# Maxout inputs of five token groups by a 3x3x2 product scheme of 15 slots a half, with nine units' keys turned on TensorE

## The chip, the cores and the metric

The kernel runs on one core of one Trainium2 chip. The metric is the device time of one execution in microseconds (us). A core has five engines that run beside each other, each through its own instruction list in order: PE (TensorE, matrix products), DVE (VectorE), ACT (ScalarE), POOL (GpSimd) and SP (SyncE, which here issues most DMAs). They wait for each other through semaphores.

## The reference

An attention recurrence in float32 over 4 batches, 8 heads, 768 steps and 48 features a head; its result, as 3072 tokens of 384 features, goes through a maxout layer:

```
f = 1 / (1 + exp(-f_logit))
for t in range(S):
    state = f[:, :, t, :, None] * state + einsum('bhd,bhe->bhde', k[:, :, t], v[:, :, t])
    y[:, :, t] = einsum('bhd,bhde->bhe', q[:, :, t], state)
x = y.transpose(0, 2, 1, 3).reshape(3072, 384)
h = maximum(maximum(x @ w1, x @ w2), x @ w3)      # w1, w2, w3: 384 x 768
out = h @ w_out                                   # w_out: 768 x 384
```

## The kernel before

**Attention.** Tokens are taken in 24 units of 128 (64 steps of two batches). A main loop makes one iteration per unit. In it stand, for the next unit n, `scan(n)` (running products `r` of the gates, DVE), `after(n)` (`ends` and the scaled keys `kh = kt * r`, POOL), `before(n)` (the scaled queries `qh`, POOL), `carry(n)` (`state` times `ends`, POOL), and the PE products of unit n-1: `y`, the state product `a<-v_ld,ks`, the pair product `a<-qh,kh` and `y<-qh,state`. The state product wants the keys with the steps on the partitions: `ks`. Units 0 to 5 get it from four PE transposes and an ACT copy (`keys`), units 6 to 21 from 16 DVE transposes of 32x128 blocks (`keys_by_blocks`, L386).

**Maxout layer.** Four units make a group of 512 tokens, packed as `xT` (384 features on 3 blocks of 128 partitions, by 512). There are six groups; the diff counts them 0 to 5, the title 1 to 6. One weight matrix is subtracted from the other two and goes into a linear part, so that `h` is the larger of two products and zero, plus the linear part. Group 0 has its own code (`ffn_first`). Groups 1 to 5 run the generator `ffn(g, xT)`: first the inputs (`inputs_by_pairs`: two products, six column blocks of 128, three feature blocks, two token halves of 256), then the outputs (`outputs_by_pairs`, `h @ w_out` by another product scheme that wants sums of `hm`, made by `sums_of_hm` on POOL). A product of 128x128 by 128x256 in float32 is two PE instructions; `inputs_by_pairs` makes 33 slots of two such products each a group, and wants five sums of pieces of `xT` (`sums_of_x`, POOL), the first of them when its sixth slot comes.

**Order.** The program is recorded in hand order, and every engine keeps to it. The main loop calls `fill(part)` five times per iteration: it advances the first generator in `pending` by nominal costs until a budget is used up. `PART` divides a group's cost over the 20 calls of four iterations, so that inputs and outputs of group g run in the iterations of group g+1's units. In an iteration about 14 slots' worth of maxout work stands around the unit's own products. `store_late` issues the stores of the group before; their source is the buffer `o` (`o_four`). SP issues, in one list, the loads of `q`, `k`, `f`, `v`, the weight checks' `raw` pieces, the stores and the copies that finish `xT`; with 16x32 pieces a unit costs many issues.

Of the kernel before, what the change touches and what calls it, by code (L numbers as in the profile page):

```python
# [46 lines left out]
C = 64  # L47
# [8 lines left out]
def kernel(  # L56
# [33 lines left out]
    def fast():  # L90
        ctx = ExitStack()
        with ctx:
# [58 lines left out]
            BY_ROWS = 6  # L151
            v_tiles = [keep.tile([128, H, DP], FP32, name=f"v_ld{i}") for i in range(NLD)]
# [52 lines left out]
            placed = [keep.tile([128, NK, 2 * PIECE], U32, name=f"placed{i}") for i in range(3)]  # L205

            def new_raw(n=0):
                n = n % RAW - (RAW - RAW_KEPT)
                if n >= 0:
                    return placed[n // NK][:, n % NK]  # L210
                return work.tile([128, 2 * PIECE], U32, name="raw", bufs=RAW - RAW_KEPT)
# [56 lines left out]
            def check_load(n):  # L268
                src = pieces[n][1]
                if src.dtype != FP32:  # L270
                    raw[n] = new_raw()
                    a = pieces[n][0].shape[1]
                    nc.sync.dma_start(out=raw[n].rearrange("p (a c) -> p a c", a=a),
                                      in_=src.bitcast(U32).rearrange("(a p) c -> p a c", a=a))
# [101 lines left out]
            def keys_by_blocks(u, n):  # L376

                if BY_ROWS <= u < NU - 2:
# [229 lines left out]
            def outputs_by_pairs(g, hm, xT):  # L608
# [13 lines left out]
                else:  # L622
# [3 lines left out]
                    partial = [rests[:, 0], rests[:, 1], rests[:, 0]]  # L626
# [170 lines left out]
            def ffn_first(xT):  # L797
# [35 lines left out]
                made += [[lambda: mix(4)]] + [[lambda n=n: mix_in(n)] for n in range(2)]  # L833
# [10 lines left out]
            w_two = [t.bitcast(FP32) for t in placed[0:2]]  # L844
            w_sum = [w_in[2][:, n] for n in range(NK)]

            def mix_in(n, engine=nc.gpsimd):

                dst, x, y, op = ((w_sum[0], w_two[1][:, 0], w_two[1][:, 1], ALU.add),
                                 (w_sum[1], w_sum[0], w_two[0][:, 0], ALU.subtract),  # L850
                                 (w_two[1][:, 0], w_two[0][:, 0], w_two[1][:, 0], ALU.subtract),
                                 (w_sum[2], w_two[0][:, 1], w_sum[1], ALU.subtract))[n]
                engine.tensor_tensor(dst, x, y, op=op)
# [3 lines left out]
            two = lambda t: t.rearrange("q (j t) -> q j t", j=2)  # L857

            def sums_of_x(g):

                if g not in summed:
                    xT = packed[g]
                    X = lambda k, h: halves(xT, k, h)
                    t1, t2, t3, t4, t5 = (halves(xT, NK, 0), halves(xT, NK, 1), s_mix[0][:, HJ - 1],
                                          rests[:, 2, 0:HALF], s_mix[1][:, HJ - 1])
                    for dst, x, y in ((t1, X(0, 1), X(0, 0)), (t2, X(1, 1), t1), (t3, X(1, 1), X(0, 1)),
                                      (t4, X(1, 0), t2), (t5, X(2, 0), X(2, 1))):
                        nc.gpsimd.tensor_tensor(dst, x, y, op=ALU.subtract)
                    summed[g] = t1, t2, t3, t4, t5
                return summed[g]  # L870

            def inputs_by_pairs(g, hm, xT):
                X = lambda k, h: halves(xT, k, h)
                t1, t2, t3, t4, t5 = sums_of_x(g)
                s1, s2, s4 = w_sum
                s3 = w_two[1][:, 0]
                COST = 2 * HALF * COLUMN
                out = lambda n, h: hm[:, 2 * n:2 * n + 2, h * HALF:(h + 1) * HALF]
                first, u3 = rests[:, 0:2, 0:HALF], tops[:, 2:4, 0:HALF]
                A, B, U5 = {}, {}, {}  # L880

                def into(b, n, w, x, begin=False):
                    for j in range(2):
                        nc.tensor.matmul(b[:, j * HALF:(j + 1) * HALF], lhsT=w[:, (2 * n + j) * 128:(2 * n + j + 1) * 128],  # L884
                                         rhs=x, start=begin and j == 0, stop=True, skip_group_check=True)

                def plain(n):
                    B[n] = bank(True)
                    into(B[n], n, w_two[0][:, 1], X(1, 0), True)
                    yield COST  # L890
                    into(B[n], n, w_two[0][:, 2], X(2, 0))
                    nc.scalar.copy(out(n, 0), two(B[n]))
                    yield COST

                def start(n):
                    A[n] = bank()
                    into(A[n], n, w_two[0][:, 0], X(0, 0), True)
                    nc.scalar.copy(first, two(A[n]))
                    yield COST

                def join(n):
                    nc.gpsimd.tensor_tensor(out(n, 0), out(n, 0), first, op=ALU.add)

                def fifth(n):
                    into(B[n], n, s1, t1, True)
                    U5[n] = two(new_top(TOK))
                    nc.scalar.copy(U5[n], two(B[n]))
                    yield COST

                def sixth(n):  # L910
                    into(A[n], n, s2, t2)
                    nc.scalar.copy(out(n, 1), two(A[n]))
                    yield COST

                def seventh(n):
                    into(A[n], n, s3, t3)
                    yield COST
# [507 lines left out]
```

## Time and profile before

| | |
|---|---|
| median of three runs | 406.75 us (406.54, 406.75, 408.45) |
| span of the profiled execution | 403.7 us |
| outside the span, by the median | 3.05 us (the profiled execution's own time isn't listed) |
| PE busy | 390.9 us, 97% of the span |
| weight loads on PE (overlap its products) | 339.7 us, 84% |
| DVE busy | 297.7 us, 74% |
| POOL busy | 256.4 us, 64% |
| ACT busy | 180.9 us, 45% |

The span runs from the first to the last instruction of the core. The page gives it in 40 slices with the busy tenths of each engine and the granted clock of PE, then the chain of work that ended last, the costliest groups of instructions (busy time, mean ns of one, idle time ahead of them and what ended it) and the DMA issues. "SPq" is SP issuing a DMA: its time is that of the issue, and the landing is told apart. A matmul's end in the timeline is modelled and overlaps the next one's start; the distance of two starts is what one costs.

### The profile page before, as it was taken

How to read it: one execution, taken by the hardware profiler on the slowest of the kernel's cores; microseconds unless marked ns; L12 is line 12 of the kernel's file. 1: busy time of each engine (PE TensorE's matmuls, PEld its weight loads, DVE VectorE, ACT ScalarE, POOL GpSimd, SP SyncE). 2: the span in 40 equal slices, each digit the busy share in tenths (PEclk: the TensorE clock that was granted, in tenths of full speed). 3: DMA queues.
4: the chain of work that ended last, by engine and by line, in shares of the span. 5: the costliest groups of instructions: out<-in, count | busy, mean ns of one | idle time of the engine just before them, and what ended most of it. 6: DMA issues, size and time to landing. Idle time of an engine off the chain costs nothing.

```text
span 403.7 us, 11683 instructions
## 1 busy us (share of the span) xinstructions
PE 390.9 (97%) x4658; PEld 339.7 (84%) x4658; DVE 297.7 (74%) x572; ACT 180.9 (45%) x431; POOL 256.4 (64%) x283
## 2 busy tenths in 40 slices
PE   5988999999999999999999999999999999999995
PEld 4766765559998889998889988899988889988995
DVE  6997897999989999897998997998995450002600
ACT  3478787422224442345532344523354425586120
POOL 2189695879997697296587277667477850435700
PEclk9999999999999999999999999999999999999999
DMA  8999986767574576576635477634573003541002
GB/s 171 233 282 284 279 214 89 153 92 150 82 96 114 69 154 135 104 120 84 131 104 97 62 113 88 156 78 81 75 157 91 1 19 87 143 136 70 2 19 63
DMA packets 181611, 47.21 MB, mean 117 GB/s; under 512 B 160497, under 2 KB 179249, under 8 KB 181553
## 3 DMA queue, kind: packets, MB, share of 16 engines
q1 hardware_dynamic: 177536, 45.52, 54.7%
q10 hardware_dynamic: 4016, 0.91, 1.1%
q8 instruction: 37, 0.61, 0.6%
q14 instruction: 22, 0.17, 0.1%
HBM read 37.75 MB, written 4.72 MB: 105 GB/s over the span
## 4 chain that ended last, share of the span: by engine, by line
PE 90%; SPq 4%; DMA 1%; ACT 1%; issue 1%; POOL 1%; DVE 0%
PE p L884 20%; PE p L633 18%; PE tr L884 16%; PE tr L633 14%; PE p L546 7%; PE y L419 3%; PE p L787 3%; PE a L400 2%; PE y L508 2%; PE a L437 2%; SPq L178 2%; DMA v_ld<-in_v_dram 1%; SPq L164 1%; SPq L222 1%; PE tr L295 1%
## 5 line engine op out<-in xcount | busy, mean ns | idle before, releaser
L386 DVE STREAM_TRANSPOSE ks<-kh 32x128 f32<-32x128 f32 x256 | 77.5, 303 | 11.5 <-POOL kh L344 7.4
L884 PE MATMUL tr<-xT,placed 128*128 128x256 f32 x180 | 44.4, 384 | 0.0
L343 POOL COPY ends<-r 128x8 f32<-128x8 f32 x24 | 8.6, 358 | 48.1 <-DVE r L333 48.1
L884 PEld LDWEIGHTS tr<-xT,placed 128*128 128x128 f32 x180 | 33.5, 190 | 4.9
L344 POOL TENSOR_TENSOR kh<-kt,r 128x512 f32<-128x512 f32 x18 | 31.9, 1772 | 8.5 <-DVE kt L300 8.5
L333 DVE TENSOR_TENSOR_SCAN r<-gate,from_one 128x520 f32<-128x520 f32 x24 | 33.2, 1382 | 5.4 <-ACT gate L312 2.8
L546 PE MATMUL p<-xT,w_in 128*128 128x256 f32 (+1 forms) x108 | 33.9, 458 | 3.0 <-POOL w_in L756 1.9
L597 POOL TENSOR_TENSOR w_in<-hm 128x256 f32<-128x256 f32 x18 | 13.3, 737 | 32.2 <-DVE hm L935 29.4
L515 ACT COPY xT<-y 64x256 f32<-64x256 f32 (+1 forms) x60 | 22.1, 368 | 22.4 <-PE y L508 21.7
L351 DVE TENSOR_TENSOR_SCAN prod<-gate,from_inv 128x520 f32<-128x520 f32 x24 | 31.6, 1317 | 0.0
L884 PE MATMUL tr<-xT,w_in 128*128 128x256 f32 x120 | 30.8, 379 | 0.0
L641 DVE TENSOR_TENSOR o<-tr,w_in 128x384 f32<-128x384 f32 (+1 forms) x11 | 5.7, 521 | 33.4 <-PE tr L633 29.0
L884 PE MATMUL p<-w_in,placed 128*128 128x256 f32 x120 | 30.4, 382 | 0.0
L633 PE MATMUL p<-placed,hm 128*128 128x192 f32 x144 | 29.7, 333 | 0.0
L546 PEld LDWEIGHTS p<-xT,w_in 128*128 128x128 f32 x108 | 19.5, 190 | 12.0 <-issue 6.0
L884 PE MATMUL p<-xT,placed 128*128 128x256 f32 x120 | 29.2, 379 | 0.0
L633 PE MATMUL tr<-w_out,w_in 128*128 128x192 f32 x144 | 28.6, 326 | 0.0
L927 DVE TENSOR_TENSOR hm<-tr,hm 128x512 f32<-128x512 f32 x15 | 10.3, 684 | 22.8 <-PE tr L884 15.9
L262 POOL TENSOR_TENSOR w_in<-top_bits,rest_bits 128x384 uint32<-128x384 uint32 x18 | 21.7, 1216 | 7.2 <-DVE top_bits L256 4.3
L884 PEld LDWEIGHTS p<-w_in,placed 128*128 128x128 f32 x120 | 22.4, 190 | 4.4 <-issue 1.5
L638 ACT COPY w_in<-p 128x384 f32<-128x384 f32 x15 | 7.2, 479 | 41.0 <-PE p L633 41.0
L284 ACT ACTIVATE raw<-top_bits 128x384 f32<-128x384 f32 x48 | 25.2, 526 | 0.4
(168 smaller groups left out, 995.6 us busy)
## 6 DMA issues: line engine op xcount, KB each, us to landing
raw<-in_moe_w_dram SPq DMA_DIRECT2D x24, 384.0 KB, 4.4
v_ld<-in_v_dram SPq DMA_DIRECT2D x48, 96.0 KB, 3.4
placed<-in_moe_w_dram SPq DMA_DIRECT2D x12, 384.0 KB, 6.3
out_dram<-o SPq DMA_DIRECT2D x45, 96.0 KB, 2.2
placed<-in_moe_w_out_dram SPq DMA_DIRECT2D x6, 384.0 KB, 5.4
f_ld<-in_f_logit_dram SPq DMA_DIRECT2D x36, 64.0 KB, 2.7
k_ld<-in_k_dram SPq DMA_DIRECT2D x36, 64.0 KB, 2.5
q_ld<-in_q_dram SPq DMA_DIRECT2D x36, 64.0 KB, 2.6
```

The source lines that it names most:

```text
L262: nc.gpsimd.tensor_tensor(dst, by(top), by(rest), op=ALU.add)
L284: nc.scalar.activation(over, size, AF.Relu, scale=(-1 / HI_MIN, 1.0)[step - 1], bias=(1.0, -HI_END * (1 - 2.0 ** -24))[step - 1], accum_ou ...
L333: nc.vector.tensor_tensor_scan(r[:, 0:LEN][:, ::-1], flat(gate)[:, ::-1], flat(from_one)[:, ::-1], 1.0, op0=ALU.mult, op1=ALU.max)
L344: (nc.vector if u < BY_ROWS else nc.gpsimd).tensor_tensor(kh.rearrange("p h a t -> p a h t"), kt, by_batch(r[:, 1:LEN + 1].rearrange("p (x ...
L351: nc.vector.tensor_tensor_scan(flat(prod), flat(gate_tiles[u % 2]), flat(from_inv[u % 2]), 1.0, op0=ALU.mult, op1=ALU.max)
L386: nc.vector.transpose(ks[n * 32:(n + 1) * 32, :, par, e0:e0 + 32], kh[p0:p0 + 32, :, a, t0:t0 + 32])
L419: nc.tensor.matmul(y[o:o + DP, a, hp * C:(hp + 1) * C], lhsT=v_ld[s, 2 * hp + par, :], rhs=d["at"][s, par, hp, :], start=(hp == 0), stop=F ...
L515: nc.scalar.copy(xT[o, :, t0 + a * C:t0 + (a + 1) * C], y[i, a, 0:HP * C].rearrange("p (h t) -> p h t", h=HP))
L546: nc.tensor.matmul(p if w < TOK else p.rearrange("p (two t) -> p two t", two=2), lhsT=w_in[i][:, kt, j * 128:(j + 1) * 128], rhs=x[:, t.st ...
L597: engine.tensor_tensor(dst, x, y, op=op)
L633: nc.tensor.matmul(b[:, p * HD:(p + 1) * HD], lhsT=x, rhs=w, start=id(b) not in begun, stop=True, skip_group_check=True)
L884: nc.tensor.matmul(b[:, j * HALF:(j + 1) * HALF], lhsT=w[:, (2 * n + j) * 128:(2 * n + j + 1) * 128], rhs=x, start=begin and j == 0, stop= ...
```

## The change

For groups 1 to 5 `inputs_by_pairs` gives way to `inputs_by_triples`: for each T in 0, 1 (three of the six column blocks) 15 slots of two products, 30 a group. It wants ten sums of `xT` instead of five, of which A1 takes the sixth, G1 the ninth and G2 the tenth. The chains A, G and C each keep one PSUM bank, to which the slots are added one after the other; ACT copies the bank after nearly every slot, and the next slot of the chain waits for that copy. For T = 1 the copies of A3, G3 and A4 go to `spare_room`, which is `o_four`, the buffer that the stores read. `sums_of_hm` runs once after T = 0 and twice after T = 1. The weights are mixed in 34 steps, 4 of them during group 0 and 30 while group 1 runs, on POOL and DVE in turn. `store_late` stands at the third slot of T = 0, in group 1 at the last one. For the units 8 to 12, 14, 16, 18 and 20 `keys_by_blocks` makes four PE transposes and an ACT copy instead of 16 DVE ones. `PART` counts 30 slots instead of 33.

```diff
+            BY_PRODUCT = [*range(2 * GRP, 3 * GRP), *range(3 * GRP, NU - 2, 2)]
...
             def keys_by_blocks(u, n):
-                if BY_ROWS <= u < NU - 2:
+                if u in BY_PRODUCT:
+                    if n == 0:
+                        kh, t = ready[u]["kh"], room_of_pairs()[:, 0].rearrange("s (hp d) -> s hp d", hp=HP)
+                        for hp in range(HP):
+                            nc.tensor.transpose(t[:, hp], kh[:, hp].rearrange("p a t -> p (a t)"), ident)
+                        ready[u]["ks"] = work.tile([UT, H, DP], FP32, name="ks")
+                        nc.scalar.copy(ready[u]["ks"].rearrange("s h d -> s (h d)"), t.rearrange("s hp d -> s (hp d)"))
+                elif BY_ROWS <= u < NU - 2:
...
+            def mix_in(T, n, engine=nc.gpsimd):
+                if n == 0:
+                    negate(T)
+                dst, x, y, plus = MIXES[n]
+                engine.tensor_tensor(W[T][dst], W[T][x], W[T][y], op=ALU.add if plus else ALU.subtract)
...
             def sums_of_x(g):
...
-                    for dst, x, y in ((t1, X(0, 1), X(0, 0)), (t2, X(1, 1), t1), (t3, X(1, 1), X(0, 1)),
-                                      (t4, X(1, 0), t2), (t5, X(2, 0), X(2, 1))):
-                        nc.gpsimd.tensor_tensor(dst, x, y, op=ALU.subtract)
+                    for n, (dst, x, y, plus) in enumerate((
+                            ("e", "x20", "x21", 0), ("a4", "x10", "e", 0), ("a5", "x11", "a4", 0), ("a2", "x01", "a5", 1),
+                            ("a3", "x10", "x20", 0), ("a1", "a2", "a3", 1), ("g3", "x00", "e", 0), ("g4", "g3", "x01", 0),
+                            ("g1", "g4", "x11", 0), ("g2", "x20", "x00", 0))):
+                        X[dst] = s_mix[0][:, 1] if dst == "a1" else free.pop()
+                        (nc.vector if g == 1 and n % 2 else nc.gpsimd).tensor_tensor(
+                            X[dst], X[x], X[y], op=ALU.add if plus else ALU.subtract)
...
+            SLOTS = (("A1", "A", "a1"), ("G1", "10", "g1"), ("M0", "F", "x00"), ("A2", "01", "a2"), ("G2", "B", "g2"),
+                     ("C1", "02", "x21"), ("A3", "C", "a3"), ("G3", "D", "g3"), ("C2", "22", "e"), ("A4", "E", "a4"),
+                     ("G4", "20", "g4"), ("M2", "12", "x10"), ("A5", "21", "a5"), ("G5", "00", "x01"), ("A6", "11", "x11"))
+
+            def inputs_by_triples(g, hm, xT):
+                X = sums_of_x(g)
...
+                spare_room = o_four.rearrange("t u c -> t (u c)")
+                left = [(T, n) for T in range(2) for n in range(len(MIXES))][4:] if g == 1 else []
+                for T in range(2):
+                    rooms = [hm[:, 3 + n] if T == 0 else spare_room[:, n * TOK:(n + 1) * TOK] for n in range(3)]
...
+                    for n, (slot, w, x) in enumerate(SLOTS):
+                        for _ in range(1 if n % 3 else 2):
+                            if left:
+                                m = len(left)
+                                mix_in(*left.pop(0), engine=nc.vector if m % 2 else nc.gpsimd)
...
+                        for i in range(2):
+                            nc.tensor.matmul(b[:, i], lhsT=W[T][w][:, i], rhs=X[x], start=chain not in begun and i == 0,
+                                             stop=True, skip_group_check=True)
...
+                        elif slot == "A3":
+                            a3 = both_w(rooms[1])
+                            nc.scalar.copy(a3, b)
+                            add(a3, a3, g1)
+                            most(0, 0, a2)
...
+                        elif slot == "G5":
+                            add(a1, b, a1, nc.vector)
+                            most(0, 1, a1)
+                            most(2, 1, g4)
+                        else:
+                            a6 = rooms[0][:, 0:HALF]
+                            nc.scalar.activation(a6, b[:, 0], AF.Relu)
+                            nc.vector.tensor_tensor(out(1, 1), b[:, 1], a6, op=ALU.max)
+                            if T == 0:
+                                sums_of_hm(hm, 0)
+                            else:
+                                for jj in (1, 2):
+                                    sums_of_hm(hm, jj)
+                        if n == (14 if g == 1 else 2) and T == 0:
+                            store_late()
...
-            PART = (33 * TOK + 64 * HD) * COLUMN / (5 * GRP)
+            PART = (30 * TOK + 64 * HD) * COLUMN / (5 * GRP)
```

In the pieces of order below, a row is the line, the operation, the names of output and inputs, and the shape. L609, L348, L349, L360, L366, L713 and L903 of the changed kernel are L597, L343, L344, L355, L361, L701 and L868 of the kernel before.

SP's list about the stores of group 0, which are issued while group 1 runs; before:

```order
L164 DMA v_ld_129<-in_v_dram 64x8x48 x2
L273 DMA raw<-in_moe_w_dram 128x3x256
L164 DMA v_ld_126<-in_v_dram 64x8x48 x2
L564 DMA out_dram<-o 64x384 x8
L273 DMA raw<-in_moe_w_dram 128x3x256
L528 DMA xT_146<-xT_146 16x3x384 x2
```

and in the changed kernel:

```order
L165 DMA v_ld_129<-in_v_dram 64x8x48 x2
L278 DMA raw<-in_moe_w_dram 128x3x256
L576 DMA out_dram<-o 64x384 x8
L165 DMA v_ld_126<-in_v_dram 64x8x48 x2
L278 DMA raw<-in_moe_w_dram 128x3x256
L540 DMA xT_146<-xT_146 16x3x384 x2
```

The eight stores move ahead of one pair of `v` loads; all that stands ahead of these rows is as it was.

ACT's list in group 1, T = 1, in the changed kernel: the copies of A1 and G1 (`hm`), A2, G2 (`top`), C1 (`hm`), then of A3, G3 and A4, with the copy of turned keys between them. Nothing in the kernel before writes a slot into `o`.

```order
L952 COPY hm<-p 128x2x256
L954 COPY hm<-tr 128x2x256
L287 ACTIVATE top_bits<-raw 128x384
L959 COPY top<-p 128x512
L963 COPY top<-tr 128x512
L289 ACTIVATE raw,outside<-top_bits 128x384
L966 COPY hm<-p 128x512
L969 COPY o<-p 128x512
L974 COPY o<-tr 128x512
L389 COPY ks<-a 128x512
L979 COPY o<-p 128x512
```

The copies of A3, G3 and A4 now write the buffer that the stores of the group before read, and the copy of unit 11's turned keys stands behind two of them.

POOL's list from the end of group 2's inputs on (the iteration that prepares unit 16), and on to the start of group 3's; before, with the sums of `hm` (L597), `ends`, `kh`, `qh` and `state` of unit 16, then those of unit 17 with a finished output part (`o`) between, and the sums of `xT` (L868):

```order
L597 TENSOR_TENSOR hm<-hm 128x2x128
L597 TENSOR_TENSOR w_in_64<-hm,w_in_64 128x256
L343 COPY ends<-r_103 128x8
L344 TENSOR_TENSOR kh<-kt,r_103 128x2x4x64
L355 TENSOR_TENSOR qh<-qt,prod 128x512
L361 TENSOR_TENSOR state<-st_141,ends 128x384
L343 COPY ends<-r_104 128x8
L344 TENSOR_TENSOR kh<-kt,r_104 128x2x4x64
L355 TENSOR_TENSOR qh<-qt,prod 128x512
L701 TENSOR_TENSOR o<-top_bits,w_in_63 128x2x192
L361 TENSOR_TENSOR state<-st_142,ends 128x384
L868 TENSOR_TENSOR xT_147<-xT_147 128x256 x2
```

and in the changed kernel, the first stretch:

```order
L935 TENSOR_TENSOR top<-top 128x512
L609 TENSOR_TENSOR w_in_64<-hm 128x256
L609 TENSOR_TENSOR w_in_64<-w_in_64,hm 128x256
L609 TENSOR_TENSOR hm<-hm 128x2x128
L609 TENSOR_TENSOR w_in_64<-hm,w_in_64 128x256
L609 TENSOR_TENSOR w_in_64<-hm 128x256
L609 TENSOR_TENSOR w_in_64<-w_in_64,hm 128x256
L609 TENSOR_TENSOR hm<-hm 128x2x128
L609 TENSOR_TENSOR w_in_64<-hm,w_in_64 128x256
L348 COPY ends<-r_103 128x8
L349 TENSOR_TENSOR kh<-kt,r_103 128x2x4x64
```

Eight sums of `hm` instead of four now stand at the end of the inputs ahead of `ends` and `kh`. The second stretch, in the changed kernel:

```order
L360 TENSOR_TENSOR qh<-qt,prod 128x512
L713 TENSOR_TENSOR o<-top_bits,w_in_63 128x2x192
L366 TENSOR_TENSOR state<-st_142,ends 128x384
L903 TENSOR_TENSOR w_in_64<-xT_147 128x256
L903 TENSOR_TENSOR w_in_64<-xT_147,w_in_64 128x256
L903 TENSOR_TENSOR xT_147<-xT_147,w_in_64 128x256
L903 TENSOR_TENSOR xT_147<-xT_147 128x256
L903 TENSOR_TENSOR top_bits<-xT_147 128x256
L903 TENSOR_TENSOR w_in_64<-xT_147,top_bits 128x256
L903 TENSOR_TENSOR top_bits<-xT_147,w_in_64 128x256
L903 TENSOR_TENSOR rest_bits<-top_bits,xT_147 128x256
```

Ten sums of `xT` stand where five stood (two more rows follow); the sixth, `a1`, is the input of the group's first slot, where before the first six slots took `xT` itself but for one.

PE's list at the end of group 1's inputs in the changed kernel (the iteration that prepares unit 12), some outputs after the last two slots: outputs of the linear part (`xT`) and of `hm`, the turning of unit 12's keys, and the first outputs that take sums of `hm` (`w_in_64`).

```order
L645 MATMUL p<-w_in_63,xT_147 128x192
L645 MATMUL tr<-w_out,hm 128x192 x2
L645 MATMUL tr<-w_in_63,xT_147 128x192
L645 MATMUL p<-w_out,hm 128x192 x2
L387 MATMUL a<-ident,kh 128x128 x4
L645 MATMUL tr<-w_out,hm 128x192 x2
L645 MATMUL tr<-w_out,w_in_64 128x192 x2
```

The transposes of `kh` stand amid the iteration's outputs; before, PE first took `kh` in the next iteration's `a<-qh,kh`.

192 lines of the change are left out of this document (88 added, 104 removed), and 4 rows, old and new, of the table MIXES.

## The prediction

> **What bounds the kernel now.** I read the page first: the totals and the granted clock.
>
> ```profile
> span 403.7 us, 11683 instructions
> PE 390.9 (97%) x4658; PEld 339.7 (84%) x4658; DVE 297.7 (74%) x572; ACT 180.9 (45%) x431; POOL 256.4 (64%) x283
> PEclk9999999999999999999999999999999999999999
> PE 90%; SPq 4%; DMA 1%; ACT 1%; issue 1%; POOL 1%; DVE 0%
> ```
>
> PE is busy 97% of the span and is 90% of the chain that ended last. The windows show that this is no average over unlike stages: where the new scheme starts (group 1) PE never rests, while POOL and DVE each lack a few us.
>
> ```profile
> 0.00:20.00 20.00, 15.03 (x223) 12.40 (x226) 16.46 (x29) 7.21 (x12) 4.20 (x27) 1.00 0.92 203
> 140.00:160.00 20.00, 19.99 (x224) 18.13 (x223) 19.20 (x37) 5.71 (x14) 16.34 (x18) 1.00 0.72 144
> ```
>
> So less work on PE shortens the time one for one, and each new wait of PE lengthens it one for one. The question is which of the two the change brings more of. The chain gives prices on PE:
>
> ```profile
> 42.24 0.66 PE tr L295 x4
> 116.11 0.86 PE p L884 x4
> 117.84 0.62 PE y L419 x32
> 119.84 2.79 PE tr L884 x12
> 127.05 2.59 PE tr L884 x12
> 174.87 0.86 PE p L884 x4
> ```
>
> A slot (four instructions) is 0.864 us (2.59 for three). A unit's own products take 2.0 (117.84 to 119.84). Group 1's inputs begin at 116.11, group 2's at 174.87.
>
> **Slots removed.** Three a group in five groups, all on PE's path: 15 x 0.864 = **-13.0**.
>
> **Keys turned on PE.** Nine times four transposes of 128x128; four such with an ident took 0.66 in the chain. 9 x 0.66 = **+5.9** (6.5 by the 4.3 us that six such turnings were busy in the second row below). What it removes, 144 DVE transposes of 303 ns, is 43.6 us of DVE's time, worth nothing of itself on a bound PE; it serves below.
>
> ```profile
> L386 DVE STREAM_TRANSPOSE ks<-kh 32x128 f32<-32x128 f32 x256 | 77.5, 303 | 11.5 <-POOL kh L344 7.4
> L371 PE MATMUL tr<-ident,kh 128*128 128x128 f32 x24 | 4.3, 308 | 0.2 <-DVE kh L344 0.2
> ```
>
> **The stores of group 0.** In group 1, T = 1, ACT copies A3, G3 and A4 into the buffer that the stores of group 0 read. The slot A4 adds to the bank that A3's copy reads, so PE waits for that copy, and the copy for the stores. SP's timeline:
>
> ```profile
> 145.70 0.61 SPq L273 DMA_DIRECT2D raw<-in_moe_w_dram  x1
> 146.41 1.29 SPq L164 DMA_DIRECT2D v_ld<-in_v_dram  x2
> 147.80 5.90 SPq L564 DMA_DIRECT2D out_dram<-o  x8
> 153.75 0.59 SPq L273 DMA_DIRECT2D raw<-in_moe_w_dram  x1
> out_dram<-o SPq DMA_DIRECT2D x45, 96.0 KB, 2.2
> L892 ACT COPY hm<-tr 128x512 f32<-128x512 f32 x15 | 8.8, 585 | 9.6 <-PE tr L884 9.5
> ```
>
> The rows abut: SP issues without a pause, so the change moves these stores only by the one pair of `v` loads that they pass: 146.41 + 5.90 = 152.3, landed 2.2 later at 154.5, copied 0.585 later: 155.1. PE, unhindered, comes to A4 of T = 1 at 116.11 + 24 slots (20.7) + two units (4.0) + two turnings between (1.3) = 142.2, and 1.3 later for the turnings of units 8 and 9 ahead: 143.5. The wait is 155.1 - 143.5 = **+11.6**. Behind A4 on PE stands all else, and behind the copy on ACT stand unit 11's `ks` and the later slots' copies. Earlier waits in group 1 (late sums, and 30 weight mixes on POOL and DVE) would only shorten this one: until 155.1 they are free. SP doing better is the one way down: 0 if the stores landed 12 us sooner, for which no row speaks.
>
> **The end of a group's inputs.** Units 12, 16 and 20 have their keys turned just after the inputs of groups 1, 2 and 3 end. DVE's, POOL's and PE's timelines of that place in group 1 (its unit's `y` at 147.31; I write y+ for the distance to it):
>
> ```profile
> 147.31 0.69 PE L419 MATMUL y<-at,v_ld 64*64 64x64 f32 x32
> 148.28 0.66 PE L400 MATMUL a<-qh,kh 48*64 48x64 f32 x32
> 155.69 1.18 PE L633 MATMUL p<-w_out,hm 128*128 128x192 f32 x4
> 150.35 0.69 DVE L403 TENSOR_TENSOR at<-a,mask 128x512 f32<-128x512 f32 x1
> ...
> 154.83 0.21 DVE L336 RECIPROCAL from_inv<-r 128x8 f32<-128x8 f32 x1
> 154.95 0.68 DVE L934 SCALAR_TENSOR_TENSOR hm<-hm,p 128x512 f32<-128x512 f32 x1
> 155.54 0.69 DVE L935 SCALAR_TENSOR_TENSOR hm<-hm,top_bits 128x512 f32<-128x512 f32 x1
> 156.38 0.78 POOL L597 TENSOR_TENSOR w_in<-hm 128x256 f32<-128x256 f32 x1 [2.72 <-PE p L633]
> 157.23 0.79 POOL L597 TENSOR_TENSOR w_in<-w_in,hm 128x256 f32<-128x256 f32 x1
> 157.99 1.72 POOL L597 TENSOR_TENSOR hm<-hm 128x256 f32<-128x256 f32 x1
> 159.67 0.73 POOL L597 TENSOR_TENSOR w_in<-hm,w_in 128x256 f32<-128x256 f32 x1
> 160.34 0.39 POOL L343 COPY ends<-r 128x8 f32<-128x8 f32 x1
> 160.69 1.36 POOL L344 TENSOR_TENSOR kh<-kt,r 128x512 f32<-128x512 f32 x1
> ```
>
> Now `kh` is ready at 162.05, y+14.7, and nobody minds. The transposes stand in PE's list behind the two outputs of the row at 155.69, so PE will want `kh` at about 156.3 (0.65 for such a row undisturbed), y+9.0. What `kh` waits for: DVE's unit work from mask to reciprocal (150.35 to 154.95 = 4.6, of which 1.26 is transposes that still stand there for groups 2 and 3), beginning at best when `a` is made (148.94, y+1.6); then the last add (0.68) and three smaller maxes (about 0.35 each, half a 512-wide one): `hm` at y+7.9. POOL then makes eight sums instead of four, at least 8 x 0.73 = 5.8, `ends` 0.35 and `kh` 1.36: y+15.4. The wait is 6.4 in groups 2 and 3, 5.1 in group 1 (no transposes): **+17.9**. From below, `kh` would have to be 6 us sooner for no wait, which the four extra sums alone (2.9) exclude; from above, sums at the mean of the four rows (1.0) give 2.2 more each, 24.5. I take the lower, since DVE has less to do beside them.
>
> The Trainium skill ("GPSIMD Engine Reference", section 8, Key points) says that GpSimd's SBUF interfaces are shared with VectorE, with contention when a DVE instruction has two SBUF inputs; the trace agrees so far as the same sum took 0.73 and 1.72 within 3 us. By that rule, since the maxes and adds moved to DVE have two inputs, the upper price (24.5) would hold and the sum end 6.6 us higher.
>
> **The start of groups 2, 3 and 4.** A1 takes the sixth sum of `xT`; before, the first five slots took none. PE's, DVE's and POOL's timelines at group 2's start, and the sums' row among the groups:
>
> ```profile
> 162.66 0.69 PE L419 MATMUL y<-at,v_ld 64*64 64x64 f32 x32
> 166.50 0.69 DVE L403 TENSOR_TENSOR at<-a,mask 128x512 f32<-128x512 f32 x1
> 171.88 2.02 POOL L344 TENSOR_TENSOR kh<-kt,r 128x512 f32<-128x512 f32 x1 [0.64 <-DVE kt L300]
> 175.97 0.84 POOL L361 TENSOR_TENSOR state<-st,ends 128x384 f32<-128x384 f32 x1
> 176.76 1.54 POOL L868 TENSOR_TENSOR xT<-xT 128x256 f32<-128x256 f32 x2
> L868 POOL TENSOR_TENSOR w_in<-xT 128x256 f32<-128x256 f32 x10 | 7.4, 740 | 0.0
> ```
>
> The sums began at 176.76, y+14.1, behind `kh`, which waited for DVE. Unit 12's transposes leave DVE: its mask can start at y+1.6 instead of y+3.8, and four more transposes (1.28) go behind it, so all comes 3.5 sooner: y+10.6. Six sums at 0.74 are 4.4: a1 at y+15.0. PE wants it at 174.87, y+12.2. Wait 2.8, three times: **+8.4** (0 if POOL also skips its slower `kh`, 12 if DVE's relief is not passed on to `kh`).
>
> **The rest.** A slot of a chain must wait for ACT's copy of the one before. With one other slot between (0.864) and a copy of 0.585, 0.28 is left for two handovers; only A5 to A6 is so close, ten times in all. With it go keys of other units and the last group: **+3** as ten times 0.3, bounds 0 and 6. The eight-sum ends of groups 4 and 5 turn no keys; stores of groups 1 to 4 are issued at the third slot, early enough by 10 us in group 4, barely in 2 and 3. The 43.6 us freed on DVE cover the mixes and maxes there.
>
> Sum on the span: -13.0 + 5.9 + 11.6 + 17.9 + 8.4 + 3 = +33.8. 403.7 + 33.8 = 437.5; with the 3.05 by which the median of the runs lies above the span (the profiled execution's own time isn't given), **441**.
>
> **Rivals.**
> *Only the stores bind.* The freed DVE time and PE's wait in group 1 put `hm` and `kh` ahead of PE for good, and the later waits vanish: -13.0 + 5.9 + 11.6 + 3 = +7.5, 414. For it: 16.34 and 19.20 busy of 20 leave room once 43.6 us go from DVE. Against: the end of the inputs is a chain that starts from the unit's products on PE, not a matter of load.
> *Faster.* The same, and the stores early too: if SP's rows abut because a full queue holds it, and not because an issue takes that long, then a freer machine issues the stores sooner. From a wait under 4.1 on (stores landed by 147) the time falls below before; with none it is 403.7 - 13.0 + 5.9 + 3 + 3.05 = 402.7, or 400 with no handovers either. For it: the DMA engines were busy 0.72 in the window from 140 to 160, the fullest of their windows quoted here after the first. Against: the stretch ahead of the stores is as full of issues after the change as before.
> *A colder clock.* A PE that stands may be granted less clock when it goes on. In this trace the clock is 1.00 even in the first 20 us, where PE was busy 15.03, and 0.98 in the last:
>
> ```profile
> 380.00:403.70 23.70, 19.55 (x120) 18.52 (x118) 4.46 (x9) 2.55 (x6) 3.84 (x5) 0.98 0.16 35
> ```
>
> These speak against it, but none follows a gap amid the kernel. If the clock fell to half after each of the four waits above 5 us (11.6, 5.1, 6.4, 6.4), and came back after as long a stretch of work as the smallest of them, 5.1, each would cost 2.55 and the time be 441 + 10 = 451. The Trainium skill ("TensorE: Matmul & The Clock Gate", Part 1) has such a rule: half clock after an idle window of about 3.4 us, until one busy window has passed; by its figure the four cost an estimated 1.7 each, 448 in all. The trace neither confirms nor refutes it, since PE has no such gap in it after its start.
>
> **How the numbers follow.** The sum as worked out 0.57; only the stores bind 0.18; a colder clock, or the slower POOL sums, 0.15; faster 0.06; near 406.75, where the stores' wait is 4 us and the later ones vanish, 0.04. From 414 to 458: the lower end is the store case, the upper the sum with the upper prices (6.6 for the sums, 3.6 for the starts, 3 for the rest, 441 + 13) and some of the clock's 10. About 0.5%, 2 us, is what a measurement can tell from no change: faster 0.06, same 0.04, slower 0.90.
>
> **What would show it.** PE's busy time falls by about 7 us while the span grows; gaps of PE appear at slot A4 of group 1 (about 11, released through ACT by the stores), ahead of the transposes of units 12, 16, 20 (5 to 7, released by `kh`) and at A1 of groups 2 to 4 (about 3, by POOL's sums); SP's stores of group 0 start at 146.4. If the first gap is missing, the stores were earlier than SP's rows say, and the time falls by its size; if those at the keys are missing, `hm` was ready sooner than y+7.9; a clock row below 0.95 in the groups would make the third rival right.

## The result, and the profile after

The changed kernel takes 483.55 us (482.25 to 485.8, four runs) where the kernel before takes 406.64 beside it: 1.190 times as long, interval 1.185 to 1.194, 77 us more. The direction was forecast, the size was not: 441 with a range up to 458. The profiled execution took 485.8, of which 484.1 are its span.

The page of the changed kernel, totals and granted clock:

```profile
span 484.1 us, 11724 instructions
PE 408.1 (84%) x4634; PEld 348.7 (72%) x4634; DVE 298.0 (62%) x502; ACT 203.5 (42%) x479; POOL 308.6 (64%) x339
PEclk9998999999979897989995799999698998999999
```

PE is no longer the bound: 76.0 us of the span it stands, against 12.8 before. And it is busy 17 us longer with fewer slots, because the clock row has 5s to 8s in it, where before it had 9s throughout. PE's waits, as the view of waits adds them up (us in total, times, longest):

```profile
PE a L387 <- POOL kh L349: 22.0, 6, 7.1
PE tr L645 <- DVE hm L932: 13.0, 4, 5.1
PE p L948 <- POOL w_in L903: 9.0, 3, 3.0
PE y L520 <- ACT seen L438: 4.9, 4, 1.5
PE p L948 <- DVE w_both L886: 3.9, 1, 3.9
PE p L948 <- POOL w_both L886: 2.4, 2, 2.2
PE p L948 <- DVE w_in L903: 1.2, 1, 1.2
```

The first row is the turning of keys (L387), the second the outputs' wait for the last maxes, the third the wait of slot A1 for the sums of `xT`, the fourth the unit's products for a small copy of ACT's, the fifth and sixth the slots' waits for mixed weights, the last group 1's A1. None is for the stores. What the clock took is worked out from windows of 1 us: PE's busy time times what the granted clock lacks to 1, summed, is 21.2 us (0.0 before). The granted clock is 1.00 or 0.50 in these traces; what lies between is a mean. Three of the windows of 20 us:

```profile
120.00:140.00 20.00, 14.98 (x185) 12.40 (x184) 13.41 (x21) 6.36 (x13) 14.43 (x17) 0.90 0.63 106
240.00:260.00 20.00, 13.12 (x179) 11.21 (x178) 15.60 (x33) 5.26 (x14) 9.61 (x10) 0.88 0.32 57
260.00:280.00 20.00, 14.29 (x184) 13.48 (x183) 6.91 (x10) 4.86 (x12) 8.34 (x10) 0.69 0.07 21
```

The first numbers behind the length are PE busy, PE's weight loads, DVE, ACT and POOL; then the clock. At the end of group 2's inputs (240 to 280) PE stands 12.6 of 40 us, and its clock is 0.88 and 0.69. No other engine is full there either: this is a chain of waits, not a lack of capacity. The place in detail, PE's rows first, then DVE's, then POOL's:

```profile
242.37 0.69 PE L431 MATMUL y<-at,v_ld 64*64 64x64 f32 x32
243.34 0.66 PE L412 MATMUL a<-qh,kh 48*64 48x64 f32 x32
257.90 1.01 PE L645 MATMUL tr<-w_out,hm 128*128 128x192 f32 x2 [5.12 <-DVE hm L932]
266.54 1.12 PE L387 MATMUL a<-ident,kh 128*128 128x128 f32 x4 [5.71 <-POOL kh L349]
243.88 0.43 DVE L932 SCALAR_TENSOR_TENSOR hm<-top 128x256 f32<-128x256 f32 x1 [4.22 <-POOL o L935]
246.21 1.25 DVE L398 STREAM_TRANSPOSE ks<-kh 32x128 f32<-32x128 f32 x4
248.22 2.28 DVE L932 SCALAR_TENSOR_TENSOR hm<-o 128x256 f32<-128x256 f32 x2
251.80 0.69 DVE L415 TENSOR_TENSOR at<-a,mask 128x512 f32<-128x512 f32 x1
257.76 0.41 DVE L1000 TENSOR_TENSOR hm<-p,o 128x256 f32<-128x256 f32 x1
242.57 1.28 POOL L935 TENSOR_TENSOR o<-o,hm 128x512 f32<-128x512 f32 x1
257.99 0.72 POOL L609 TENSOR_TENSOR w_in<-hm 128x256 f32<-128x256 f32 x1 [7.77 <-DVE hm L932]
265.32 1.17 POOL L349 TENSOR_TENSOR kh<-kt,r 128x512 f32<-128x512 f32 x1
```

PE made `a` by 244.0 (y+1.6), but DVE came to the mask only at 251.80 (y+9.4): it had stood 4.22 for an add of POOL's and then worked off adds, maxes and unit 15's transposes. So `hm` was ready at 258.2, y+15.8, the sums began behind it, and `kh` came at 266.5, y+24.1. PE waited twice, 5.12 for `hm` and 5.71 for `kh`.

### The profile page after: what moved, and what is told of

Read it like the earlier page. It is cut to its first block, busy times and chain, and to the rows that moved or that the text cites. A ratio compares the mean times of both kernels' runs of the same rounds, so it can differ in the third digit from the quotient of the medians.

```text
span 484.1 us, 11724 instructions
## 1 busy us (share of the span) xinstructions
PE 408.1 (84%) x4634; PEld 348.7 (72%) x4634; DVE 298.0 (62%) x502; ACT 203.5 (42%) x479; POOL 308.6 (64%) x339
## 5 line engine op out<-in xcount | busy, mean ns | idle before, releaser
L348 POOL COPY ends<-r 128x8 f32<-128x8 f32 x24 | 7.2, 301 | 69.5 <-DVE r L338 69.5
L948 PE MATMUL p<-xT,w_both 128*128 128x256 f32 x160 | 43.5, 396 | 3.9 <-POOL w_both L886 2.2
L415 DVE TENSOR_TENSOR at<-a,mask 128x512 f32<-128x512 f32 x24 | 16.5, 687 | 43.4 <-PE a L412 43.3
L948 PEld LDWEIGHTS p<-xT,w_both 128*128 128x128 f32 x160 | 30.7, 196 | 10.5 <-ACT top L991 3.3
L349 POOL TENSOR_TENSOR kh<-kt,r 128x512 f32<-128x512 f32 x18 | 31.3, 1739 | 10.0 <-DVE kt L305 10.0
L398 DVE STREAM_TRANSPOSE ks<-kh 32x128 f32<-32x128 f32 x112 | 33.9, 303 | 3.3 <-POOL kh L349 1.6
L645 PE MATMUL tr<-w_out,w_in 128*128 128x192 f32 x144 | 32.1, 355 | 0.0
L527 ACT COPY xT<-y 64x256 f32<-64x256 f32 (+1 forms) x60 | 22.1, 368 | 23.4 <-PE y L520 22.6
L609 POOL TENSOR_TENSOR w_in<-hm 128x256 f32<-128x256 f32 x18 | 13.4, 745 | 28.7 <-DVE hm L932 21.9
L932 DVE SCALAR_TENSOR_TENSOR hm<-top 128x256 f32<-128x256 f32 x20 | 10.8, 542 | 32.5 <-POOL hm L935 16.5
L645 PE MATMUL tr<-w_out,hm 128*128 128x192 f32 x72 | 19.4, 385 | 13.2 <-DVE hm L932 13.0
L935 POOL TENSOR_TENSOR top<-top 128x512 f32<-128x512 f32 x20 | 26.8, 1342 | 4.8 <-ACT top L963 3.9
L645 PEld LDWEIGHTS tr<-w_out,w_in 128*128 128x128 f32 x144 | 27.7, 213 | 0.0
L387 PE MATMUL a<-ident,kh 128*128 128x128 f32 x36 | 7.6, 349 | 22.0 <-POOL kh L349 22.0
```

The costliest lines, as they stand in the source:

```text
L349: (nc.vector if u < BY_ROWS else nc.gpsimd).tensor_tensor(kh.rearrange("p h a t -> p a h t"), kt, by_batch(r[:, 1:LEN + 1].rearrange("p (x ...
L398: nc.vector.transpose(ks[n * 32:(n + 1) * 32, :, par, e0:e0 + 32], kh[p0:p0 + 32, :, a, t0:t0 + 32])
L415: nc.vector.tensor_tensor(at, p[:, :, 0:HP * C].rearrange("s par (h t) -> s par h t", h=HP), mask.unsqueeze(1).unsqueeze(1).to_broadcast([ ...
L527: nc.scalar.copy(xT[o, :, t0 + a * C:t0 + (a + 1) * C], y[i, a, 0:HP * C].rearrange("p (h t) -> p h t", h=HP))
L645: nc.tensor.matmul(b[:, p * HD:(p + 1) * HD], lhsT=x, rhs=w, start=id(b) not in begun, stop=True, skip_group_check=True)
L935: engine.tensor_tensor(dst, x, y, op=ALU.add)
```

## The experiments

Each is timed against the kernel before on the same chip; "the changed kernel" is the 483.55 one.

### Idle work ahead of the waits: the clock

```diff
+                        for m in range({12: 36, 16: 20, 20: 20}.get(u, 0)):
+                            nc.tensor.transpose(t[:, m % HP], ident, ident)
                         for hp in range(HP):
                             nc.tensor.transpose(t[:, hp], kh[:, hp].rearrange("p a t -> p (a t)"), ident)
...
+                        if slot == "A1" and T == 0 and g > 1:
+                            for m in range(6):
+                                nc.tensor.matmul(b[:, m % 2], lhsT=ident, rhs=X["x00"], start=True, stop=True, skip_group_check=True)
```

> The changed kernel with idle work for PE put ahead of the waiting instructions: 36, 20 and 20 transposes of the identity ahead of the keys of units 12, 16 and 20, six products of 128x256 ahead of A1 in groups 2 to 4; they write banks that are overwritten next, and the result is the same. Theory A (PE's clock falls to half because PE stands): the half-clock stretches after these waits go (1.85, some 2.5, 2.56, and 1.7 after two of the A1s), the waits stay as long, the mean clock rises from 0.94 to 0.96 or more, time about 474 (471 to 478). Rival B (the clock falls for another reason): clock 0.94, time 483 to 487.

It took 477.93, 5.6 less, with 124 more instructions on PE. Its mean clock (the view of cores):

```profile
core 0: 479.6 us, clock 0.964
```

By the same sum of windows the clock cost 15.3 instead of 21.2. The difference of 5.9 is close to the time gained, 5.6 by the medians (4.5 by the spans of the two profiled executions). The idle work has nothing to do but keep PE moving, so theory A holds in kind; forecast 474, it was 3.9 too hopeful, since the gaps that were not filled (the waits for `hm`) still start half-clock stretches (254 to 261, 333 to 340).

### No mixes in group 1: the wait for the stores

```diff
-                left = [(T, n) for T in range(2) for n in range(len(MIXES))][4:] if g == 1 else []
+                left = [(1, 6), (1, 2)] if g == 1 else []
```

> The changed kernel with 28 of the 30 weight mixes of group 1 left out (the result is then not the reference's). Theory A (mixing holds PE in group 1, and the wait for the stores of group 0 lies just under it): the waits of 3.87 and 2.19 and their half clock go, PE comes to slot A4 of T = 1 at about 151.5 and waits there for the stores, which land at about 154.8: A4 at 155.4 instead of 161.4, and the time 477.5 (475 to 480). Rival B (the mixes' load is felt later too, by the end of group 1's inputs and after): 470 or less. Rival C (the store wait isn't there): 474, with no gap at A4.

475.07, between A's 477.5 and B's 470. The mixes' waits are gone, and the wait that the prediction had counted on comes to light. SP's row of the stores and PE's row of A4, and below them the same two rows of the changed kernel:

```profile
147.94 5.05 SPq L576 DMA_DIRECT2D out_dram<-o  x8
155.45 2.07 PE L948 MATMUL p<-w_in,extra 128*128 128x256 f32 x4 [4.43 <-ACT o L969]
147.07 5.39 SPq L576 DMA_DIRECT2D out_dram<-o  x8
162.33 1.03 PE L948 MATMUL p<-w_in,extra 128*128 128x256 f32 x4
```

A4 at 155.4 as forecast, through ACT's copy into `o`. In the changed kernel the same stores went out from 147.07 to 152.46, but PE came to A4 only at 162.3, held by waits and clock, without a wait there: the stores had landed. Leaving out the mixes gains 8.5, with 4.4 of this wait in their place.

### Keys: all back on DVE, all on PE, and alone in the kernel before

```diff
-            BY_PRODUCT = [*range(2 * GRP, 3 * GRP), *range(3 * GRP, NU - 2, 2)]
+            BY_PRODUCT = []
```

> The changed kernel with no keys turned on TensorE (the list of units is empty; DVE turns them all as before). Theory A (each wait of PE is a chain at its place: kh behind eight sums behind a late hm): the 22.0 us of waits for kh shrink to some 7, since two outputs later PE wants the fifth of those sums anyway; the 5.9 us of turnings go, and with them some 5 of half clock; DVE's 16 blocks come back into the iterations of units 12, 16 and 20 and make the A1 waits of groups 2 to 4 longer by 3.5 each (3.0 to 6.5), and hm in group 1 later by up to 5. Sum about -11: 472 (460 to 485). Rival B (load: what mattered was the 43.6 us taken from DVE): 490 or more.

489.04, 5.5 more than the changed kernel: outside A's range and 1 short of B's, so nearer to B. The waits for `kh` are gone altogether, but the others grew:

```profile
PE p L948 <- POOL w_in L903: 18.2, 3, 6.4
PE tr L645 <- DVE hm L932: 15.4, 3, 5.1
```

A1's wait doubled (6.1 a time, where theory A had said 6.5), and group 1's sums, the mixes and some slots were waited for longer, in part at places that had been free. So theory A priced the starts right and missed what DVE's transposes do to the work within a group.

```diff
+            BY_PRODUCT = [*range(2 * GRP, NU - 2)]
```

> The changed kernel with the keys of units 13, 15, 17, 19 and 21 turned on TensorE too: 80 more DVE transposes (24 us) gone, 3.3 us more on PE. Theory A (hm comes late at the end of groups 2 and 3 because DVE has unit 15's and 19's transposes, 5 us, among the last maxes): hm and the sums behind it come about 4 us sooner there, waits for hm fall from 5.1 to about 1, less half clock, some 0.5 us of new waits a unit: 475 (470 to 479). Rival B (POOL's adds set hm, DVE waits 4.2 for one of them): hm as late as now, 486 to 490.

470.31, 13.2 less: A, and more than it said.

```profile
PE a L387 <- POOL kh L349: 26.5, 6, 7.1
PE tr L645 <- DVE hm L932: 3.7, 4, 2.3
```

The waits for `hm` fell from 13.0 to 3.7. PE then stands before the turning instead, 7.1 in each of the three groups, which is the eight sums and `kh` seen from `hm`: a chain that DVE's relief doesn't shorten. The clock's cost fell to 16.4.

The third kernel is the one before, with the nine units' keys turned on PE and nothing else:

```diff
+            BY_PRODUCT = [*range(2 * GRP, 3 * GRP), *range(3 * GRP, NU - 2, 2)]
...
             def keys_by_blocks(u, n):
-                if BY_ROWS <= u < NU - 2:
+                if u in BY_PRODUCT:
...
+                elif BY_ROWS <= u < NU - 2:
```

> The kernel before, with nothing changed but that the keys of the same nine units are turned on TensorE. Theory A (chains at places: PE takes kh some 9 us behind the unit's y, and kh of units 8 to 12, 16 and 20 is ready only 11 to 15 behind it): 5.9 of turnings, some 20 of waits for kh, 4 of half clock: 435 (420 to 442). Rival B (the nine turnings cost little by themselves, the relieved DVE makes kh early, and the cost is the 3x3x2 scheme's): 410 to 415.

431.96 (1.064, 1.060 to 1.068): A. One row of waits carries it:

```profile
PE a L383 <- POOL kh L345: 15.4, 5, 4.7
```

15.4 of waits, 5.9 of turnings and 4.7 of clock make 26.0, and 25.9 were measured. So the two halves of the change don't add: turning keys on PE costs 26 us in the old scheme and gains 5.5 in the new one, where DVE is what the maxes and adds wait for.

### The turning one fill later

```diff
                 if u in BY_PRODUCT:
-                    if n == 0:
+                    if n == 1:
```

> The changed kernel with the nine turnings one fill later in the same iteration (some 3 us of PE's work later, behind the first outputs that take sums of hm). Theory A (kh behind all eight sums is what is late; the outputs behind it need only the fifth sum, 4 us sooner): the waits for kh go from 22 to about 7 in all, with some 4 of half clock: 465 (459 to 472). Rival B (the wait only moves to the sums or to the next unit's a): 478 to 484.

466.68, 16.9 less: A within 2 us.

```profile
PE tr L645 <- DVE hm L932: 13.0, 4, 5.1
PE a L387 <- POOL kh L349: 6.9, 4, 1.8
```

The waits for `kh` fall from 22.0 to 6.9 and those for `hm` stay to the tenth; the clock's cost falls from 21.2 to 12.9. Of these 23.4 the span shows 19.1 (484.1 to 465.0), since small waits for ACT's and DVE's results grew elsewhere.

### The three reliefs together

```diff
+            BY_PRODUCT = [*range(2 * GRP, NU - 2)]
...
-                    if n == 0:
+                    if n == 1:
...
-                        (nc.vector if g == 1 and n % 2 else nc.gpsimd).tensor_tensor(
+                        (nc.vector if n % 2 else nc.gpsimd).tensor_tensor(
```

> The changed kernel with keys of all units from 8 to 21 turned on TensorE, one fill later, and the ten sums of xT shared by DVE and POOL in every group. Theory A: on 470.3 of the kernel with all keys on TensorE, some 16 less of waits for kh, 1.5 less at each of three A1s, 5 less of half clock: 445 (437 to 456). Rival B: the waits move to the next step: 462 to 470.

446.39: A. What is left of waits is spread over every step:

```profile
PE p L948 <- DVE w_in L903: 7.3, 4, 2.0
PE a L387 <- POOL kh L349: 6.9, 4, 1.8
PE tr L645 <- POOL w_in L609: 5.3, 3, 1.8
```

Most are below 2 us, and the clock's cost is down to 4.5. It is still 40 us slower than the kernel before: of the 40.4 on the span (444.1 against 403.7) 37.7 are more standing of PE and 4.5 the clock, less 1.8 of work. What would take away that standing, no run shows.

### The new scheme in the last group alone

Beside the last group's inputs no unit's work runs. Groups 1 to 4 keep `inputs_by_pairs`, all keys from unit 6 on stay with DVE; the weights, which the pairs scheme needs until group 4's inputs end, are mixed while its outputs run. The changed kernel's weight buffers come with it and are left out here.

```diff
             def ffn(g, xT):
                 hm = new_hm()
-                yield from inputs_by_pairs(g, hm, xT)
-                yield from outputs_by_pairs(g, hm, xT)
+                yield from inputs_by_triples(g, hm, xT) if g == LAST else inputs_by_pairs(g, hm, xT)
+                if g == LAST - 1:
+                    nc.vector.tensor_tensor(w_two[1][:, 0], w_two[0][:, 0], w_two[1][:, 0], op=ALU.subtract)
+                    left = [(T, n) for T in range(2) for n in range(len(MIXES))]
+                    for cost in outputs_by_pairs(g, hm, xT):
+                        for _ in range(2):
+                            if left:
+                                mix_in(*left.pop(0), engine=nc.vector if len(left) % 2 else nc.gpsimd)
+                        yield cost
+                else:
+                    yield from outputs_by_pairs(g, hm, xT)
```

> The kernel before, with the new scheme in the last group alone, where no unit's work runs beside the inputs: groups 1 to 4 keep 33 slots, all keys from unit 6 on turned by DVE, the weights mixed on DVE and POOL while group 4's outputs run. Theory A (the three slots are worth their 2.6 us where DVE and POOL are free): 404.5 (403 to 406). Rival B (mixes, ten sums and copies between the slots of a chain cost as much as the slots even there): 406.5 to 410.

410.22 (1.010, 1.007 to 1.013): B, 0.2 above its range. One wait after the start-up, and 1.67 of half clock behind it:

```profile
PE p L977 <- DVE w_in L932: 4.1, 1, 4.1
```

It is A1's, for sums of `xT` that stood behind the mixes on both engines. The next kernel takes the sums on DVE alone, ahead of T = 1's mixes, which run beside T = 0's slots:

```diff
-                        (nc.vector if n % 2 else nc.gpsimd).tensor_tensor(
+                        nc.vector.tensor_tensor(
...
-                left = []
+                left = [(1, n) for n in range(len(MIXES))] if g == LAST else []
...
-                    left = [(T, n) for T in range(2) for n in range(len(MIXES))]
+                    left = [(0, n) for n in range(len(MIXES))]
...
-                        for _ in range(2):
-                            if left:
-                                mix_in(*left.pop(0), engine=nc.vector if len(left) % 2 else nc.gpsimd)
+                        if left:
+                            mix_in(*left.pop(0), engine=nc.vector)
```

> As the kernel with the new scheme in the last group alone, which took 410.2 with one gap of 4.11 at the last group's A1 and 1.67 of half clock behind it. Here the 17 mixes for T = 1 are made while T = 0 runs, and the ten sums of xT on DVE alone, ahead of them. Theory A (that gap is all that stands against the 2.6 us of the three slots): no gap at A1, clock 1.00, 404.4 (403.5 to 405.5), about 0.4% under the kernel before. Rival B (the gap comes back at another step: T = 1's mixed weights late, or the copies between slots): 406 to 409.

407.72 (1.004, 1.003 to 1.006): B again. The gap at A1 is gone, and another stands in T = 1, where a slot waits for a bank that DVE's add, behind mixes, had not read yet:

```profile
PE tr L977 <- DVE hm L964: 2.6, 1, 2.6
```

So both halves of the mixes go into group 4's outputs, T = 0's on DVE and T = 1's on POOL:

```diff
-                left = [(1, n) for n in range(len(MIXES))] if g == LAST else []
+                left = []
...
-                        if left:
-                            mix_in(*left.pop(0), engine=nc.vector)
+                        if left:
+                            _, n = left.pop(0)
+                            mix_in(0, n, engine=nc.vector)
+                            mix_in(1, n)
```

> As the kernel before it (new scheme in the last group alone, 407.7 with one gap of 2.56 in T = 1 behind the mixes that share DVE and POOL with the slots' adds, and 1.71 of half clock), with all 34 mixes made while group 4's outputs run: T = 0's on DVE, T = 1's on POOL, the sums of xT on DVE behind them. Theory A (mixing beside the slots held DVE and POOL): no gap above 0.5 after 60 us, clock 1.00, 403.5 (402.5 to 404.5), some 0.6% under the kernel before. Rival B (DVE doesn't finish mixes and sums by A1 at 349, a gap there again): 406 to 410.

405.38 (0.998, 0.997 to 1.000): between the two. The clock stays at 1.00, but A1 still waits 1.5, since DVE was slow at its mixes. The mixes' rows (ns, shortest, median, longest):

```profile
PE p L977 <- DVE w_in L932: 1.5, 1, 1.5
L897 DVE TENSOR_TENSOR w_both<-w_both x11: 832/941/1237, 331.4 to 347.5; 128x256 f32<-128x256 f32 x11
L897 POOL TENSOR_TENSOR w_both<-w_both x11: 789/902/907, 332.9 to 348.1; 128x256 f32<-128x256 f32 x11
```

Both engines took some 0.9 a mix while they ran side by side. The last kernel gives all 34 to DVE:

```diff
-                    left = [(0, n) for n in range(len(MIXES))]
+                    left = [(T, n) for T in range(2) for n in range(len(MIXES))]
...
-                        if left:
-                            _, n = left.pop(0)
-                            mix_in(0, n, engine=nc.vector)
-                            mix_in(1, n)
+                        for _ in range(2):
+                            if left:
+                                mix_in(*left.pop(0), engine=nc.vector)
```

> As the kernel with all 34 mixes made while group 4's outputs run (405.4, with a gap of 1.49 at the last group's A1 behind DVE). There DVE and POOL shared them, and while both ran a mix took 0.94 on DVE and 0.90 on POOL. Here DVE makes all 34 and POOL none. Theory A (the two engines slow each other: a mix alone on DVE takes 0.42): 34 x 0.42 = 14.3 instead of 16, the sums of xT are done by 348, no gap at A1, 403.7 (403 to 404.5). Rival B (a mix takes DVE some 0.9 whatever POOL does): 34 x 0.9 = 31 us, A1 waits some 10, 416.

403.73 (403.2 to 404.99): 0.994 of the kernel before, interval 0.992 to 0.996: a small gain, but one clear of the noise, and less time than either kernel takes.

```profile
PE 387.7 (97%) x4646; PEld 336.7 (84%) x4646; DVE 323.1 (80%) x628; ACT 185.4 (46%) x442; POOL 258.8 (64%) x282
L897 DVE TENSOR_TENSOR w_both<-w_both x22: 412/422/1244, 330.7 to 345.9; 128x256 f32<-128x256 f32 x22
```

From the first mix's start to the last one's end DVE alone needs 15.6 us (330.7 to 346.3) where the two engines needed 17.5 (331.4 to 348.9), and PE waits nowhere after the start-up. The three slots saved are then worth their 2.6 us (2.7 by the medians).

## Why the prediction was right in direction and wrong in size

On the span the forecast was +33.8; it became +80.4: 63.2 more of standing and 21.2 of clock, less 4.0 of work (PE's 408.1 less the 21.2 is 386.9, against 390.9). The 3.05 that the forecast adds for what lies outside the span is 1.7 in the profiled execution (485.8 less 484.1).

- **Work on PE** (-13.0 + 5.9 = -7.1): measured -4.0. What the other 3 are is open; ends of matmuls beside gaps are modelled.
- **The clock** (nothing in the sum; "a colder clock" was a rival, which shared 0.15 with slower POOL sums, at 10 us): 21.2. This is the largest miss of a single term, and the failed step is that it was put at nothing, on a trace without gaps amid the kernel. The rival, right in kind, counted four waits of over 5 us with 2.55 each. In truth stretches of half clock also began at waits of 3.9, 3.0 and 2.2, at two places even at 1.3 and 1.5, and in group 2 the two waits of the inputs' end fell into one stretch of 17 us. Filling gaps gave time back at about the rate of the clock's loss.
- **The stores of group 0** (+11.6): SP issued them from 147.07 to 152.46 where 146.4 to 152.3 was forecast, but the term was not what PE waited for. It reached A4 at 162.3 through waits that the prediction had called free until 155.1: 2.4 for unit 8's keys, 1.2 at A1, 6.6 for mixes, and half clock behind them; some 3 more had gone before group 1 (a wait of 1.3 for ACT at 41.7 and half clock behind it). The step that failed is "earlier waits would only shorten this one": together they outgrew it. With the mixes out, the wait stood there with 4.43. The mechanism was real, its place on the path was not.
- **The end of a group's inputs** (+17.9): 36.1 (18.6 for `kh`, 13.0 for `hm`, 4.5 for ACT's `seen` and DVE's `o` just ahead). The failed step is "beginning at best when `a` is made": I put DVE's unit work at y+1.6, `hm` at y+7.9 and `kh` at y+15.4; they came at y+9.4, y+15.8 and y+24.1. The prices were near (from mask to `hm` 6.4 where 6.3 was forecast, from `hm` to `kh` 8.3 where 7.5 was); what was missing is that DVE, in order, has adds and maxes of the slots of T = 1 and unit 15's transposes ahead of the unit's mask, and that these wait for POOL's adds, which stand among POOL's own unit work. The second failed step is that PE would reach the turning at y+9.0: outputs ahead of it take `hm` themselves, and it came at y+18.5. That the waits for `kh` alone, 18.6, lie near the 17.9 is therefore luck: `kh` and PE were late by about as much, 8.7 and 9.5. That DVE's load was in this chain is shown by the kernel with all keys on PE (waits for `hm` 13.0 to 3.7), that the turning's place in PE's list was, by the later turning (waits for `kh` 22.0 to 6.9).
- **The start of groups 2 to 4** (+8.4): 9.0, three times 3.0 where 2.8 was forecast. Right, step by step: in group 2 the sums began at y+10.5, `a1` was ready at y+15.2 and PE came at y+12.2, against y+10.6, y+15.0 and y+12.2.
- **The rest** (+3): 7.9 as the remainder of the standing: the wait for ACT ahead of group 1, group 4's and 5's and the small waits, not taken apart further.
- **Only the stores bind** and **faster**: false. Even with the three reliefs together the kernel takes 446.

The 43.6 us taken from DVE I had called worth nothing of itself. In the old scheme that is so. In the new one it was worth 5.5 us net of 5.9 for the turnings and 22.0 of waits for them, since DVE had become part of the chain.

The Trainium skill ("TensorE: Matmul & The Clock Gate", Part 1) says that the clock is half or full, and changes by windows of about 3.4 us. The trace agrees: these runs have no clock but 1.00 and 0.50, and the time at half clock per stretch comes to 3.41 or 6.83 in nearly every stretch, at most to 17.07, five times 3.41. Its price of an estimated 7 us for four waits was short because more waits tripped it, and some for several windows on end.

## What to carry to other kernels

When a change takes slots from a full engine and gives adds, maxes and copies to the others, price it by the in-order lists of those others: find what stands ahead of the first thing that the full engine wants, and follow it back through both engines, from the moment at which each is really free and not from the moment at which its input is there. Add for each new wait of about 3 us or more a further 1.7 for the clock as an estimate; one of the three A1 waits cost nothing more. And try such a scheme first where nothing runs beside it: here it lost 77 us in five groups, with the nine units' keys on PE, and gained 2.7 in one.

## What the runs showed of the hardware

**A wait costs twice, or not, by where it falls.** In the trace of the changed kernel the clock changes only at points that lie 3.41 us or a multiple of it apart, so the time falls into fixed stretches. These are the stretches about the three A1 waits of groups 2 to 4, of 3.01, 3.00 and 3.01 us, which ended at 210.29, 291.07 and 369.99 (PE busy behind the length, the clock third from the end):

```profile
207.60:211.02 3.42, 0.73 (x3) 0.68 (x4) 1.56 (x5) 0.00 (x0) 3.18 (x6) 1.00 0.76 91
211.02:214.43 3.41, 3.41 (x106) 2.82 (x108) 0.00 (x0) 0.73 (x2) 2.10 (x3) 0.50 0.98 187
286.11:289.52 3.41, 1.96 (x13) 1.67 (x11) 1.28 (x4) 0.91 (x3) 3.17 (x6) 1.00 0.78 95
289.52:292.94 3.42, 1.87 (x58) 1.49 (x60) 0.49 (x2) 0.63 (x2) 3.18 (x6) 1.00 0.73 132
368.03:371.44 3.41, 1.45 (x28) 1.07 (x32) 0.88 (x3) 0.24 (x1) 3.24 (x5) 1.00 0.74 93
371.44:374.85 3.41, 3.41 (x120) 3.27 (x110) 1.16 (x3) 0.83 (x3) 1.42 (x2) 0.50 0.83 231
```

In the first wait PE stood 2.69 of one stretch, in the third 1.96, and the next stretch was at half clock, which cost 1.7. The second lay across two stretches with 1.45 and 1.55 of standing, and the clock stayed. Between 50 and 400 us of this execution every stretch at full clock with 1.96 or more of standing was followed by half clock, and none with 1.85 or less; outside of that, 1.46 and 1.53 were enough at two places and 2.33, in the start-up, was not, so the amount alone doesn't decide it everywhere.

**DVE and POOL slow each other.** A 128x256 float32 mix with two inputs in memory takes 0.42 on DVE alone and 0.94 while POOL makes such mixes; POOL takes 0.90 then, where it took 0.73 for its sums of that size in the kernel before. The last kernel shows it in one place, where POOL's sums end at 332.2:

```profile
331.32 0.91 POOL L609 TENSOR_TENSOR w_in<-hm,w_in 128x256 f32<-128x256 f32 x1
331.56 0.94 DVE L897 TENSOR_TENSOR w_in<-w_both 128x256 f32<-128x256 f32 x1
332.43 0.41 DVE L897 TENSOR_TENSOR extra<-w_both 128x256 f32<-128x256 f32 x1
```

The Trainium skill ("SBUF — State Buffer", SBUF: two separate sides) calls the ports that both use an exclusive lock for such instructions, held for a whole instruction. The runs agree that sharing such work gains nothing (17.5 against 15.6 us); but instructions that fully exclude each other would make a pair an estimated 0.42 + 0.73 = 1.15, and a pair took 0.9, so a part of it seems to overlap.
